# Pooled attention and a gated FFN on one core: the first keys and queries loaded by SyncE as float32 and cast on the engines, conv weights by ScalarE's queue, wrap copies over two blocks, and a new order

## The chip, the cores and the metric

The kernel runs on one core of one Trainium2 chip. The metric is the device time of one execution in microseconds (us). Three runs of the kernel before gave 217.94, 218.74 and 219.59 us.

## The reference, cut to what matters

Shapes: q, k, v are float32 [8, 8, 576, 64] (batch, heads, sequence, head size); the FFN has `w_in` [512, 1024], `conv_w` [3, 1024], `w_out` [1024, 512]; the result is float32 [8, 576, 512].

```python
# attention over keys and values that are averaged in groups of 8 positions
k_p = k.reshape(B, H, 72, 8, D).mean(axis=3)
v_p = v.reshape(B, H, 72, 8, D).mean(axis=3)
scores = scale * q @ k_p.T
scores = scores - scores.max(-1)
attn = exp(scores) / (exp(scores).sum(-1) + 1e-9)
x = (attn @ v_p)                       # heads joined: [B, 576, 512]
# gated FFN
h = maximum(x @ w_in, 0)               # [B, 576, 1024]
conv = conv_w[0] * h[s-1] + conv_w[1] * h[s] + conv_w[2] * h[s+1]
out = (h * sigmoid(conv)) @ w_out
```

## The kernel before

The eight batches are taken in four groups of two. Each batch goes through the same stages. Its keys are pooled and turned (`prep_k` by TensorE with a pooling matrix for batches 0 and 1; `pool_pair` by VectorE adds and `turn_pair` for the later groups). Its queries are turned (`prep_q`, or a transposing DMA for the last group). Its values are pooled by VectorE (`prep_v`). Attention runs in tiles of 128 rows (`att_scores`, `att_max`, `att_shift`, `att_exp`, a turn of the exponentials, `att_values`, `att_divide`, a turn of x). Then come `ffn_in` (line 712), relu on ScalarE (721), the convolution over positions, tanh, the gate, and `ffn_out` (928) with stores. The convolution is done on TensorE by small matmuls with diagonal matrices `dw` (874) for most quarters, and on VectorE by three taps (849) for six of them.

Positions lie in a strided order (position = 9 p + c), so that the neighbour of a row is a shift by 64 columns, except at the ends of the tile. For batches 4 to 7 the two wrapped column blocks at the ends of `hT` are written by GpSimd copies (`ffn_wrap`, lines 796 and 797) so that convolution reads one straight run. `Graph.WRAPS` says for how many of the 128-channel blocks one pair of copies is done.

What sets the order: every operation is added to a graph with its engine and costs. `Graph.ORDER`, a table of numbers, is the order in which the operations are emitted; an odd number picks the second of the two engines that could do a copy. A -1 is a spare matmul on zeros (`fill`, line 384) that only keeps TensorE busy. `FORMS` picks between two matmul shapes for some operations, and `PLACES` gives each operation its buffer. Each engine then works through its own list strictly in that order, and waits by semaphores for what other engines deliver. Costs and landing times in the `add` calls serve the making of the table, which was written into the file; they are not read on the chip.

What the change touches in the kernel before:

- All q, k and v loads, `w_in` and `w_out` are issued by GpSimd, whose DMAs cast float32 to bf16 on the way (`load_heads`, line 272). The first keys come in two halves of the heads (`kk`, 128x2x576), the first queries in two parts of the columns (`qp`, 128x4x256 and 128x4x320). GpSimd also builds the mask, the identity and, by two selects of line 316, the pooling matrix `pm`, which VectorE then doubles (332).
- The conv weights are loaded by SyncE (line 297), turned by one small matmul (365), and made into `convw` and `dw` by VectorE.
- `clear_ends` (lines 791 and 792) zeroes the two outer columns of both `hT` buffers on GpSimd.

Of the kernel before, what the change touches and what calls it, by code (L numbers as in the profile page):

```python
# [33 lines left out]
class Graph:  # L34
# [27 lines left out]
    WRAPS = 4  # L62
# [60 lines left out]
    )  # L123
    FORMS = (
        0, 1, 0, 1, 0, 1, 1, 0, 0, 0, 0, 0, 1, 1, 1, 0, 0, 0, 0, 0, 0, 1, 1, 0, 0, 0, 0, 0, 0, 0, 0, 1, 1, 1, 0, 1, 1, 1, 1, 1,
    )
    PLACES = (
# [50 lines left out]
def kernel(  # L178
# [102 lines left out]
    def load_q(b, **part):  # L281
        load_heads(buf("qp", b), q, b, **part)
# [707 lines left out]
    def soon():  # L990
        seq[0] += 0.01
        return seq[0]
# [400 lines left out]
```

## Time and profile before

| | |
|---|---|
| runs of the kernel | 217.94, 218.74, 219.59 us; median 218.74 |
| the profiled execution | 219.76 us, of which the span of instructions is 218.0 us, the rest lies around it |
| mean granted TensorE clock | 0.997 |
| busy: PE, DVE, ACT, POOL | 200.7, 194.2, 158.6, 39.1 us |
| HBM read, written | 32.52 MB, 9.44 MB |

The profile is of one execution. PE is TensorE, DVE VectorE, ACT ScalarE, POOL GpSimd, SP SyncE. "Busy" is the time in which an engine had an instruction in work; matmuls overlap, so a busy PE isn't PE at its peak. "Landing" is the time from a DMA's issue to the arrival of its last data. The DMA columns give the mean busy share of the 16 DMA engines and the bytes that they wrote per second; a load that casts reads twice the bytes that it writes.

### The profile page before, as it was taken

The page shows a single profiled execution, that of the slowest core. Times are in us where ns is not written, and L with a number is a line of the kernel's source. Part 1 is how long each engine was busy: PE and PEld are TensorE (multiplying, and loading weights), DVE is VectorE, ACT ScalarE, POOL GpSimd, SP SyncE. Part 2 cuts the span into 40 slices and gives each one's busy share as a digit, 9 for nine tenths or more (in the row PEclk, how much of TensorE's full clock was granted, in tenths as well). Part 3 has the DMA queues.
Part 4 walks back from the last instruction along what each step waited for, and adds up shares of the span by engine and source line. Part 5 has one row for each costly group of instructions (what it writes and reads, how often), then busy time and mean ns, then how long its engine had stood idle before and what let it go on. Part 6 is the DMA issues. An engine that isn't in the chain of part 4 may idle for free.

```text
span 218.0 us, 6525 instructions
## 1 busy us (share of the span) xinstructions
PE 200.7 (92%) x2718; PEld 136.8 (63%) x2718; DVE 194.2 (89%) x339; ACT 158.6 (73%) x269; POOL 39.1 (18%) x65
## 2 busy tenths in 40 slices
PE   2798999997999999999999998999999999999991
PEld 1465778774688776856777765566556656654451
DVE  7569879999999998999999997999999999999531
ACT  2046676798989868867786985699599989988410
POOL 7951422042042012000000012002010120321000
PEclk9999999999999999999999999999999999999998
DMA  4999999999999999984956895476564555401886
GB/s 70 141 191 208 208 206 208 206 208 205 210 225 207 206 149 183 143 165 92 168 119 88 129 101 108 99 143 117 113 144 89 129 110 121 100 0 36 197 255 189
DMA packets 48833, 32.61 MB, mean 150 GB/s; under 512 B 28300, under 2 KB 44324, under 8 KB 48804
## 3 DMA queue, kind: packets, MB, share of 16 engines
q0 software_dynamic: 16288, 16.26, 46.3%
q1 hardware_dynamic: 31476, 14.44, 34.6%
q10 hardware_dynamic: 1040, 1.51, 2.4%
q8 instruction: 21, 0.34, 0.6%
q14 instruction: 8, 0.07, 0.1%
HBM read 32.52 MB, written 9.44 MB: 192 GB/s over the span
## 4 chain that ended last, share of the span: by engine, by line
PE 44%; DVE 31%; DMA 11%; issue 6%; POOL 5%; ACT 2%; DVEq 0%; POOLq 0%
PE psum L928 19%; PE psum L712 14%; DMA w_in_sb<-in_moe_w_in_dram 9%; DVE negm L593 6%; DVE x L682 5%; DVE sd L605 4%; PE psum L874 4%; DVE tg L849 4%; DVE gT L912 3%; PE psum L667 3%; DMA eT<-e 2%; DVE v L471 2%; DVE gT L920 2%; DVE r L680 2%; POOL qp L272 1%
## 5 line engine op out<-in xcount | busy, mean ns | idle before, releaser
L712 PE MATMUL psum<-xT,w_in_sb 128*128 128x288 bf16 x512 | 73.6, 286 | 0.8 <-DVE sd L605 0.3
L928 PE MATMUL psum<-w_out_sb,gT 128*128 128x512 bf16 (+1 forms) x296 | 69.8, 373 | 1.2 <-DVE gT L920 0.7
L712 PEld LDWEIGHTS <-w_in_sb 128*128 128x128 bf16 x512 | 47.9, 98 | 17.4 <-issue 1.0
L721 ACT ACTIVATE hT<-psum 128x576 bf16<-128x576 f32 x64 | 40.1, 651 | 12.2 <-PE psum L712 12.0
L928 PEld LDWEIGHTS <-gT 128*128 128x128 bf16 x296 | 27.3, 98 | 26.4 <-issue 1.5
L849 DVE SCALAR_TENSOR_TENSOR tg<-hT,convw,tg 128x576 f32<-128x576 bf16 x48 | 37.4, 816 | 0.5
L593 DVE TENSOR_REDUCE negm<-psum 128x8 f32<-128x576 f32 (+2 forms) x37 | 27.4, 751 | 3.2 <-PE psum L580 2.7
L682 DVE TENSOR_TENSOR x<-psum,r 128x512 bf16<-128x512 f32 (+1 forms) x37 | 25.6, 691 | 1.3
L796 POOL COPY hT<-hT 128x252 bf16<-128x252 bf16 x8 | 4.5, 559 | 100.1 <-ACT hT L721 90.9
L667 PE MATMUL psum<-vm,eT 128*128 128x130 bf16 (+5 forms) x240 | 19.2, 222 | 2.1 <-DMA eT<-e 1.3
L605 DVE TENSOR_TENSOR sd<-psum,negm 128x576 f32<-128x576 f32 x27 | 20.0, 752 | 0.5
L874 PE MATMUL psum<-hT,dw 64*64 64x288 bf16 (+2 forms) x608 | 19.3, 261 | 1.0 <-issue 0.4
L667 PEld LDWEIGHTS <-eT 128*128 128x128 bf16 (+1 forms) x240 | 15.3, 101 | 6.1 <-DMA eT<-e 1.8
L631 ACT ACTIVATE e<-sd 128x576 bf16<-128x576 f32 x27 | 18.1, 682 | 1.3 <-DVE sd L605 1.0
L874 PEld LDWEIGHTS <-dw 64*64 64x64 bf16 x608 | 15.0, 107 | 5.4 <-issue 4.2
L854 ACT ACTIVATE gT<-tg 128x576 bf16<-128x576 f32 x24 | 16.2, 687 | 2.7 <-DVE tg L849 2.6
L847 ACT ACTIVATE tg<-hT,convw 128x576 f32<-128x576 bf16 x24 | 18.0, 780 | 0.1
L939 ACT COPY osb<-psum 128x512 f32<-128x512 f32 x26 | 14.8, 587 | 4.1 <-PE psum L928 4.0
L899 ACT ACTIVATE tg<-psum 128x576 bf16<-128x576 f32 x20 | 13.0, 648 | 4.4 <-PE psum L874 3.7
L899 ACT ACTIVATE gT<-psum 128x576 bf16<-128x576 f32 x20 | 13.0, 648 | 3.4 <-PE psum L874 3.1
L920 DVE TENSOR_TENSOR gT<-gT,hT 128x2304 bf16<-128x2304 bf16 x10 | 13.5, 1351 | 0.1
L471 DVE TENSOR_TENSOR v<-v 128x1280 bf16<-128x1280 bf16 (+2 forms) x24 | 13.0, 540 | 0.1
(82 smaller groups left out, 230.2 us busy)
## 6 DMA issues: line engine op xcount, KB each, us to landing
out_dram<-osb SPq DMA_DIRECT2D x54, 128.0 KB, 2.4
v<-in_v_dram POOLq DMA_DIRECT2D x8, 512.0 KB, 14.5
qp<-in_q_dram POOLq DMA_DIRECT2D x7, 576.0 KB, 15.2
kk<-in_k_dram POOLq DMA_DIRECT2D x3, 1152.0 KB, 14.4
out_dram<-qp ACTq DMA_DIRECT2D x10, 128.0 KB, 2.8
w_in_sb<-in_moe_w_in_dram POOLq DMA_DIRECT2D x2, 512.0 KB, 17.6
w_out_sb<-in_moe_w_out_dram POOLq DMA_DIRECT2D x1, 1024.0 KB, 23.8
out_dram<-qp SPq DMA_DIRECT2D x6, 128.0 KB, 2.6
```

The lines of the kernel that those rows point to most:

```text
L593: nc.vector.tensor_reduce(out=a["m"][0:rows], in_=a["s"][0:rows, :, 0:2 * KW].rearrange("p a (h s) -> p a h s", s=Sp), axis=AX.X, op=OP.ma ...
L605: nc.vector.tensor_tensor(out=a["d"][0:rows], in0=a["s"][0:rows, :, 0:2 * KW].rearrange("p a (h s) -> p a h s", s=Sp), in1=a["m"][0:rows]. ...
L631: nc.scalar.activation(out=dst, in_=src, func=ACT.Exp, scale=1.0 / (POOL * 8.0),)
L667: nc.tensor.matmul(out=a["o"][lo:hi, h // 4, (h % 4) * (D + 1):(h % 4 + x1 - x0) * (D + 1)], lhsT=a["eT"][:, j, lo:hi], rhs=buf("vm", b)[: ...
L682: nc.vector.tensor_tensor(out=a["x"][0:rows].rearrange("p (a h d) -> p a h d", a=2, d=D), in0=ov[:, :, :, 0:D], in1=r[0:rows].unsqueeze(3) ...
L712: nc.tensor.matmul(out=banks(ps)[:, j, 0:SC], lhsT=w_in_block(dc, fb), rhs=buf("xT", g)[:, dc, i * S + j * SC:i * S + (j + 1) * SC], start ...
L721: nc.scalar.activation(out=h_of(b)[:, fb].rearrange("p (a s) -> p a s", a=2), in_=banks(ps)[:, :, 0:SC], func=ACT.Relu, scale=0.5,)
L847: nc.scalar.activation(out=acc, in_=h, func=ACT.Identity, scale=w)
L849: nc.vector.scalar_tensor_tensor(out=acc, in0=h, scalar=w, in1=acc, op0=OP.mult, op1=OP.add)
L874: nc.tensor.matmul(out=banks(pss[r ^ c])[c * D:(c + 1) * D, j, lo:hi], lhsT=dw[r * D:(r + 1) * D, tap * n_fb + fb, :], rhs=hT[r * D:(r + 1 ...
L899: nc.scalar.activation(out=t.rearrange("p (a s) -> p a s", a=2), in_=banks(ps)[:, :, 0:SC], func=ACT.Tanh, scale=0.5,)
L928: nc.tensor.matmul(out=bank(ps)[0:rows, columns], lhsT=buf("gT", g)[:, fb, t * P:t * P + rows], rhs=w_out_sb[:, fb, columns], start=(fb == 0),
```

## The change

The first keys and the first part of the first queries are no longer loaded by GpSimd. SyncE loads them uncast, as float32, into the two `hT` buffers, which are not in use yet (`load_raw`), and four copies cast them to bf16 into their old places (`cast_raw`): one half of the keys on VectorE, the other half and two halves of the query part on ScalarE. Of the first queries the second part stays with GpSimd, but waits in the graph for the pooling matrix. The conv weights are issued from ScalarE's queue and their turning matmul stands later. `clear_ends` comes after the four casts, since the staging lies in `hT`. `WRAPS` goes from 4 to 2. `ORDER`, `FORMS` and `PLACES` are new throughout.

```diff
-    WRAPS = 4
+    WRAPS = 2
...
-        24, 2, 6, 28, 36, 4, 26, 18, 8, 16, 10, -1, 14, 20, -1, -1, 34, 54, -1, 12,
+        0, 10, 12, 24, 16, -1, 4, 44, -1, 28, 8, -1, 36, -1, 14, -1, -1, 32, -1, -1,
...
+    def raw_rows(i):
+        flat = buffers["hT"][i].rearrange("p a s -> p (a s)").bitcast(FP32)
+        return flat[:, 0:H // 2 * C * D].rearrange("p (h x) -> p h x", h=H // 2)
+
+    def load_raw(i, heads, cs):
+        rows = (k, q)[i][0].rearrange("h s d -> (h s) d").rearrange("(h p c) d -> p h c d", p=P, c=C)
+        nc.sync.dma_start(
+            out=raw_rows(i)[:, heads, cs.start * D:cs.stop * D].rearrange("p h (c d) -> p h c d", d=D),
+            in_=rows[:, heads, cs],
+        )
+
+    def cast_raw(i, heads, cs, copy):
+        part = slice(cs.start * D, cs.stop * D)
+        copy(out=(k_rows_of(0), buf("qp", 0))[i][:, heads, part], in_=raw_rows(i)[:, heads, part])
...
-        nc.sync.dma_start(out=cw_raw, in_=cw)
+        nc.scalar.dma_start(out=cw_raw, in_=cw)
...
+        if b == 0 and (kind == "k" or part["cs"].start == 0):
+            heads, cs = part.get("heads", slice(0, 4)), part.get("cs", slice(0, C))
+            d = add({"SP": 0.5}, key, lambda: load_raw(raw, heads, cs), land=(0.6, kb * share, RATE_FIRST))
+            cast = []
+            for lo in range(heads.start, heads.stop, 2):
+                two, n = slice(lo, lo + 2), 2 * D * (cs.stop - cs.start)
+                o = add(either(0.145 + n * 0.00056, 0.25 + n * 0.00085), key, None, after=[d], uses=[toks[b]])
+                o.emit = lambda o=o, two=two: cast_raw(raw, two, cs, copier(o))
...
+    ends = add({"POOL": 0.8}, 0, clear_ends, after=raws)
...
-    add_load("q", 0, first("q0+"), 5 / 9, cs=slice(4, C))
+    add_load("q", 0, first("q0+"), 5 / 9, [p0], cs=slice(4, C))
```

The start of GpSimd's list, after the constants, before:

```order
6 L272 DMA kk_76<-in_k_dram 128x2x576
7 L335 MEMSET mask 128x15
8 L337 ISA
9 L337 AFFINE_SELECT mask<-mask 128x15 x2
10 L272 DMA kk_76<-in_k_dram 128x2x576
11 masks.py:197 MEMSET ident 128x128
12 masks.py:199 AFFINE_SELECT ident<-ident 128x128
13 L272 DMA qp_72<-in_q_dram 128x4x256
14 L272 DMA qp_72<-in_q_dram 128x4x320
15 L316 AFFINE_SELECT gT_120<-gT_120 64x9x72 x2
16 L290 DMA v_85<-in_v_dram 128x4x512
```

The same place after the change (line numbers of the changed kernel, where the lines from 297 on stand 15 or more further down):

```order
6 masks.py:197 MEMSET ident 128x128
7 masks.py:199 ISA
8 masks.py:199 AFFINE_SELECT ident<-ident 128x128
9 L350 MEMSET mask 128x15
10 L352 AFFINE_SELECT mask<-mask 128x15 x2
11 L331 AFFINE_SELECT gT_120<-gT_120 64x9x72 x2
12 L272 DMA qp_72<-in_q_dram 128x4x320
13 L305 DMA v_85<-in_v_dram 128x4x512
14 L308 DMA v_85<-in_v_dram 64x512
15 L272 DMA kk_76<-in_k_dram 128x4x576
16 L272 DMA qp_73<-in_q_dram 128x4x576
```

Three loads have left GpSimd's list, and the mask, identity and pooling matrix now stand ahead of its first load. Further on the first half of `w_in` stands ahead of batch 2's queries, where it stood behind them.

VectorE's list around the copy that doubles the pooling matrix, before:

```order
21 L349 TENSOR_SCALAR vm_88<-mask 128x15
22 L349 TENSOR_SCALAR vm_89<-mask 128x15
23 L349 TENSOR_SCALAR vm_90<-mask 128x15
24 L349 TENSOR_SCALAR vm_91<-mask 128x15
25 L349 TENSOR_SCALAR vm_92<-mask 128x15
26 L332 COPY gT_120<-gT_120 64x9x72
27 L354 COPY mask_wide<-mask 128x960
28 L416 COPY kT_80<-psum 64x2x72 x3
```

And after the change:

```order
15 L364 TENSOR_SCALAR vm_91<-mask 128x15
16 L364 TENSOR_SCALAR vm_92<-mask 128x15
17 L327 MEMSET kT_80 128x288
18 L369 COPY mask_wide<-mask 128x960
19 L294 COPY kk_76<-hT_114 128x1152
20 L347 COPY gT_120<-gT_120 64x9x72
21 L431 COPY kT_80<-psum 64x2x72 x2
22 L534 COPY qT_77<-psum 128x2x256
```

The wide mask and the cast of the first keys now stand ahead of the doubling copy (347, before 332), and six memsets of `e` and the four copies of `pick`, which stood ahead of it, stand behind it.

SyncE's list at its start, before:

```order
1 L297 DMA gT_120<-in_moe_conv_w_dram 24x128
2 L951 DMA out_dram<-osb_121 64x512 x2
3 L651 DMA_TRANSPOSE eT_102<-e_96 128x5x128
4 L951 DMA out_dram<-osb_122 64x512 x2
5 L513 DMA_TRANSPOSE qT_77<-qp_73 128x18x128
6 L951 DMA out_dram<-osb_123 64x512 x2
7 L651 DMA_TRANSPOSE eT_104<-e_97 128x5x128
```

And after the change:

```order
1 L287 DMA hT_114<-in_k_dram 128x2x576
2 L287 DMA hT_115<-in_q_dram 128x4x256
3 L287 DMA hT_114<-in_k_dram 128x2x576
4 L666 DMA_TRANSPOSE eT_103<-e_97 128x5x128
5 L666 DMA_TRANSPOSE eT_104<-e_96 128x5x128
6 L528 DMA_TRANSPOSE qT_77<-qp_73 128x18x128
7 L966 DMA out_dram<-osb_121 64x512 x2
8 L966 DMA out_dram<-osb_122 64x512 x2
9 L966 DMA out_dram<-osb_123 64x512 x2
```

The three new loads come first, and the first stores of results now stand behind the large transposing DMA of batch 6's queries (528, before 513).

More of the change, by code (lines that the diff above doesn't have):

```diff
@@ L70 @@
     ORDER = (
[52 rows of a table removed]
[52 rows of a table added]
     )
     FORMS = (
-        0, 1, 0, 1, 0, 1, 1, 0, 0, 0, 0, 0, 1, 1, 1, 0, 0, 0, 0, 0, 0, 1, 1, 0, 0, 0, 0, 0, 0, 0, 0, 1, 1, 1, 0, 1, 1, 1, 1, 1,
+        1, 0, 1, 0, 1, 1, 1, 0, 0, 0, 0, 1, 1, 0, 0, 1, 1, 0, 0, 0, 0, 1, 1, 0, 0, 0, 0, 1, 0, 0, 0, 1, 1, 1, 1, 0, 1, 1, 1, 1,
     )
     PLACES = (
[17 rows of a table removed]
[17 rows of a table added]
     )
@@ L983 @@
     LATE = 1.4
-    RATE, RATE_FIRST = 402e3, 341e3
+    RATE, RATE_FIRST = 402e3, 395e3
     seq = [START]
@@ L992, in soon, with add_load @@
         return seq[0]
-    loads = {}
+    loads, raws = {}, []
     kk, kp, qp, qTt = {}, {}, {}, {}
     kb = B and H * S * D * 4
-    def add_load(kind, b, key, share=1.0, **part):
-        f, toks = (load_k, kp) if kind == "k" else (load_q, qp)
+    def add_load(kind, b, key, share=1.0, after=(), **part):
+        f, toks, raw = (load_k, kp, 0) if kind == "k" else (load_q, qp, 1)
         if kind == "k":
@@ L1003, in add_load @@
             toks[b] = token("qp", b)
-        o = add({"POOL": 0.77}, key, lambda: f(b, **part), uses=[toks[b]],
-                land=(0.5 if key == first("k0") else 1.3, kb * share, RATE_FIRST) if b == 0 else (LATE, kb, RATE))
+        if b == 0 and (kind == "k" or part["cs"].start == 0):
[6 more added lines that the diff above has]
+                o.emit = lambda o=o, two=two: cast_raw(raw, two, cs, copier(o))
+                cast.append(o)
+                raws.append(o)
+            loads.setdefault((kind, b), []).append(cast if kind == "q" else cast[0])
+            return
+        o = add({"POOL": 0.77}, key, lambda: f(b, **part), uses=[toks[b]], after=after,
+                land=(1.3, kb * share, RATE_FIRST) if b == 0 else (LATE, kb, RATE))
         loads.setdefault((kind, b), []).append(o)
@@ L1009 @@
     lv, vtok, vmtok, ktok = {}, {}, {}, {}
-    ends = add({"POOL": 0.8}, 0, clear_ends)
     def add_load_v(b, key):
@@ L1025 @@
     add_load("k", 0, first("k0+"), 0.5, heads=slice(2, 4))
-    cwl = add({"SP": 0.6}, soon(), load_conv, land=(1.5, 0, 1))
+    cwl = add({"ACT": 0.6}, soon(), load_conv, land=(7.0, 0, 1))
     cb0 = add({"DVE": 0.25}, soon(), lambda: nc.vector.memset(blank, 0.0))
@@ L1140, in add_prep_q @@
                 o = add({"PE": 0.52 * n / C}, key_q + half * gap + 2.2 * part, None,
-                        after=[loads["q", b][part], c0, idf], behind=[qfirst.get(b - 1)], count=4 * n, uses=[t, qp[b], qTt[b]], mode=HALF)
+                        after=[loads["q", b][part][half] if b == 0 and part == 0 else loads["q", b][part], c0, idf], behind=[qfirst.get(b - 1)], count=4 * n, uses=[t, qp[b], qTt[b]], mode=HALF)
                 o.emit = lambda o=o, half=half, part=part, t=t: prep_q(b, half, part, t, o.mode)
```

136 rows, old and new, of tables (ORDER, PLACES) are left out of this document.

## The prediction

> **What bounds the kernel now.** I read the busy shares first, then the stages, then who was waited for in the first stage.
>
> ```profile
> PE 200.7 (92%) x2718; PEld 136.8 (63%) x2718; DVE 194.2 (89%) x339; ACT 158.6 (73%) x269; POOL 39.1 (18%) x65
> DMA  4999999999999999984956895476564555401886
> 8.00:16.00 8.00, 6.79 (x133) 4.91 (x133) 5.29 (x10) 2.59 (x5) 5.76 (x9) 1.00 1.21 177
> ...
> 24.00:32.00 8.00, 7.29 (x141) 5.52 (x140) 6.63 (x13) 5.45 (x10) 2.21 (x3) 1.00 1.24 206
> 32.00:40.00 8.00, 8.00 (x113) 6.62 (x115) 7.65 (x15) 4.99 (x8) 1.32 (x2) 1.00 1.23 207
> 40.00:80.00 40.00, 37.42 (x637) 28.77 (x626) 39.00 (x71) 36.04 (x63) 8.73 (x15) 1.00 1.20 202
> 80.00:160.00 80.00, 77.33 (x1173) 53.38 (x1173) 76.82 (x127) 60.37 (x102) 5.17 (x9) 1.00 0.77 128
> 160.00:200.00 40.00, 39.73 (x288) 24.24 (x289) 39.10 (x54) 37.75 (x64) 6.68 (x10) 1.00 0.39 88
> ```
>
> The stage rows give the window, its length, then the busy time of PE, PEld, DVE, ACT and POOL, the granted clock, the DMA share and GB/s. From 32 us to 200 us DVE is busy for 162.6 of 168 us, and PE nearly as long. There, what starts later ends later; little can be hidden. Before 32 us there are holes, and the DMA engines are full from the second slice of the span on (5 us). So the first stage is the place to look, and its question is whether data come late. The rows of the engines, each with the start and the duration, say yes:
>
> ```profile
> 10.70 0.64 PE L501 MATMUL psum<-ident,qp 128*64 128x128 bf16 x16 [0.94 <-DMA qp<-in_q_dram]
> 12.63 0.75 POOL L290 DMA_DIRECT2D v<-in_v_dram  x1
> DMA to landing us min/median/max: 20.2/20.2/20.2
> 33.23 1.71 DVE L471 TENSOR_TENSOR v<-v 128x1280 bf16<-128x1280 bf16 x3
> 20.84 1.03 POOL L279 DMA_DIRECT2D kk<-in_k_dram  x1 [4.77 <-PE psum L401]
> DMA to landing us min/median/max: 18.0/18.0/18.0
> 39.43 2.63 DVE L424 TENSOR_TENSOR kk<-kk 128x2304 bf16<-128x2304 bf16 x3
> ```
>
> The landing rows belong to the load quoted ahead of each. Batch 1's values land at 12.63 + 20.2 = 32.8, and DVE takes them up at 33.23. The second group's keys land at 20.84 + 18.0 = 38.8, and DVE takes them up at 39.43. The first queries keep PE waiting until 10.70. Up to 39 us the line of loads sets the pace, because the work that uses each load begins within 0.7 us of its landing. **If that line moves, the program moves.**
>
> **What the change does to the line of loads.**
>
> ```profile
> 1.32 0.85 POOL L272 DMA_DIRECT2D kk<-in_k_dram  x1 [0.80 <-POOLq L1377]
> 0.81 0.43 SPq L297 DMA_DIRECT2D gT<-in_moe_conv_w_dram  x1
> 1.80:2.00 0.20, 0.00 (x0) 0.00 (x0) 0.15 (x1) 0.20 (x1) 0.20 (x1) 1.00 0.22 59
> 2.80:3.00 0.20, 0.00 (x0) 0.00 (x0) 0.20 (x1) 0.00 (x0) 0.20 (x2) 1.00 0.51 46
> 3.00:9.00 6.00, 4.57 (x28) 2.20 (x29) 4.15 (x23) 0.36 (x2) 5.86 (x10) 1.00 1.02 134
> 9.00:10.00 1.00, 0.75 (x19) 0.58 (x18) 0.61 (x3) 0.21 (x1) 1.00 (x2) 1.00 1.27 167
> 206.00:208.00 2.00, 2.00 (x11) 0.87 (x9) 0.00 (x0) 1.07 (x2) 0.00 (x0) 1.00 1.00 286
> 214.00:216.00 2.00, 0.00 (x0) 0.00 (x0) 0.07 (x1) 0.00 (x0) 0.00 (x0) 1.00 0.96 316
> ```
>
> SyncE's load issued at 0.81 moved its 12 KB within 1.8 to 2.0 us (59 GB/s in that window). GpSimd's first load, issued at 1.32, moved its first data from about 2.8 us. So SyncE's loads begin about 1.0 us earlier.
>
> Now the three moved loads. As bf16 they are 2 x 295 KB and 262 KB, 0.852 MB written. Before, 6 us at 134 GB/s make 0.804 MB by 9.0, 0.009 MB came ahead of that, and the rest comes at 167 GB/s: they are through, counted by bytes, at 9.2 us. After, they are written as float32, 1.704 MB. Uncast traffic from the hardware queues is seen only at the end, in the stores: 286 to 316 GB/s with the engines full. At these rates the three take 5.4 to 6.0 us and end at 7.2 to 7.8 us, so **the line is 1.4 to 2.0 us ahead**. Bounds from other rows: a saturated casting load writes 208 GB/s and so reads 416; at 416 the three end at 5.9, 3.3 us ahead. If the written side were the limit at 208 GB/s, they would end at 10.0, 0.8 us behind; at the start's own 134 GB/s they would end at 14.5, 5.3 us behind. The stores are nearest, being uncast float32 from the same kind of queue, but they are paced by PE in part, so I take 1.9, near the upper end of theirs.
>
> [...]
>
> Does the line then run on without a hole? GpSimd builds the identity, mask and pooling matrix first:
>
> ```profile
> 2.37 0.54 POOL L337 TENSOR_SCALAR_AFFINE_SELECT mask<-mask 128x15 bf16<-128x15 bf16 x2
> 3.88 0.29 POOL masks.py:199 TENSOR_SCALAR_AFFINE_SELECT ident<-ident 128x128 bf16<-128x128 bf16 x1
> 5.63 1.92 POOL L316 TENSOR_SCALAR_AFFINE_SELECT gT<-gT 64x648 bf16<-64x648 bf16 x2
> 3.62 0.24 DVE L1027 MEMSET gT<- 128x224 uint32 x1
> 5.09 0.33 DVE L329 MEMSET gT<- 64x324 uint32 x1
> ```
>
> Identity and mask take 1.3 us with their memsets, from 1.32 to 2.6. The selects need DVE's memsets; these took 3.62 to 5.42 before, 1.8 us, and now come first on DVE, so they end at 2.7. The selects end at 4.6, and the held load of queries is issued then; first data come 1.5 us later, at 6.1, while SyncE's loads still run to 7.2 or later. So no hole. Values, batch 1's keys and queries follow at once; then GpSimd waits for the casts (the four memsets of `clear_ends`) before it issues `w_in`. The casts end near 9.5 us (below), and the loads already issued, batch 1's queries as the last of them, landed past 18 us before and move by no more than the lead, so this wait is hidden; it costs only if ScalarE's cast came 9 us later. Behind it stand `w_in` and batch 2's queries.
>
> **The engines in the first 12 us.** DVE's list now reaches the doubling of the pooling matrix like this:
>
> ```profile
> 0.93 0.82 DVE L312 MEMSET v<- 64x256 uint32 x3 [0.93 <-PEq L1377]
> 3.03 0.29 DVE L312 MEMSET e<- 128x32 uint32 x6
> 5.59 0.48 DVE L349 TENSOR_SCALAR vm<-mask 128x15 bf16<-128x15 bf16 x5
> 7.58 0.34 DVE L332 COPY gT<-gT 64x648 bf16<-64x648 bf16 x1 [1.51 <-POOL gT L316]
> 7.95 1.15 DVE L354 COPY mask_wide<-mask 128x960 bf16<-128x960 bf16 x1
> 7.98 0.93 PE L391 MATMUL psum<-gT,kk 128*64 128x144 bf16 x18 [0.51 <-DVE gT L332]
> 12.03 0.41 PE L580 MATMUL psum<-kT,qT 128*128 128x144 bf16 x4
> ```
>
> Before, DVE ran from 0.93 to 6.07 and then waited 1.51 us for GpSimd's selects. Now that wait is gone, but the wide mask (1.15) and a cast of 1152 elements stand ahead, while the memsets of `e` (0.3) and four small copies of `pick`, taken as 0.3 too, left: 6.07 - 0.6 + 1.15 = 6.6, plus the cast. No row shows a cast of float32 in SBUF. It lies between a DVE copy of 1152 elements (0.75 us, below) and the 1.15 us for 960, stretched to 1152 (1.38). I take 1.0: the doubling copy starts at 7.6, as before. **The first key matmul gains nothing.** What gains is what follows. PE needn't wait until 10.70 for queries. ScalarE's cast of the second key half (1.1 us by the copy of 1152) ends near 9.5 us, 1.3 us after its data at about 8.2; the second key matmuls follow, then 28 query turns (1.0 us). The first scores come at about 11.4 instead of 12.03.
>
> ```profile
> L519 DVE COPY qT<-psum 128x1152 bf16<-128x1152 bf16 x4 | 3.0, 751 | 0.6 <-PE psum L667 0.6
> L519 ACT COPY qT<-psum 128x1152 bf16<-128x1152 bf16 x6 | 6.7, 1122 | 0.5 <-PE psum L501 0.4
> L656 DVE COPY eT<-psum 128x640 bf16<-128x640 bf16 x5 | 2.4, 484 | 0.0
> L797 POOL COPY hT<-hT 128x252 bf16<-128x252 bf16 x8 | 6.5, 810 | 0.0
> 85.39 7.95 SPq L513 DMA_TRANSPOSE qT<-qp  x1
> ```
>
> From there to batch 1's values four copies have left DVE for ScalarE or for later: queries of 1152 columns (0.75), queries and exponentials of 640 (0.48 each), exponentials of 320 (0.3 at that rate), 2.0 us together. With the 0.6 DVE can be 2.6 us ahead at 33 us, more than the loads' 1.9, so the loads still set the pace there. Past the second group's keys the DVE lists differ by two query copies more (1.50) and four other copies less (1.6): nothing. So a lead of 1.9 us at 39 us is passed on.
>
> The conv weights now land later, but are used only after the second tile's scores; the finer wrap copies double GpSimd's count from 16 to 32 at about half the length (810 ns for 252 columns), and GpSimd is 18% busy. Both cost nothing; if GpSimd were the last to be waited for, a wrap pair would come about 0.7 us sooner.
>
> **The sum.** 1.9 us off the span of 218.0 gives 216.1, off the profiled 219.76 gives 217.9. That execution is 1.0 us above the median of the runs, so against the median: 218.74 - 1.9 = **216.8 us**.
>
> **Rivals.**
> (a) The lead grows: the loads run at 416 GB/s and the new order closes holes. The 32 to 200 us rows leave 5.4 us of DVE idle. With 3.3 us from the loads and 1 us of holes, 214.4. For it: the casting loads do read at 416. Against: the two lists have the same structure.
> (b) The float32 writes limit the start. They are twice the bytes. Below 1.704 / (9.2 - 1.8) = 230 GB/s the line falls behind; at 134 it costs 5.3 us: 224.0. For it: 134 GB/s is what this very stage shows. Against: uncast stores go at 286 or more.
> (c) A new wait at SyncE. The transposing DMA that held SyncE for 7.95 us now stands ahead of three stores, and the second of its kind ahead of two sends of exponentials. If that one too takes 7.95, both tiles come late by 0 to 7.95 us; with buffers only three deep I take a little over the middle, 4.5: 218.74 - 1.9 + 4.5 = 221.3. It decides once those sends are needed sooner than the transposing DMA ends. For it: the row above. Against: TensorE and DVE have other tiles in work.
> (d) The change doesn't move the line: DVE's start, unmoved at 7.6, bounds all tiles of batch 0. Then only the 0.6 us count: 218.1.
>
> **How the numbers follow.** Forecast 0.45, (a) 0.20, (b) 0.08, (c) 0.15, (d) 0.12. About 1% (2.2 us) is what a measurement of this kernel can tell from no change; the limits are 216.55 and 220.93. The forecast's own range is 215.4 to 218.4; a little under half of it lies below 216.55 once reordering is allowed 1 us. Faster: 0.20 + 0.20 of the forecast's 0.45 = 0.40. Slower: (b) and 0.12 of (c)'s 0.15, 0.20. Same: the other 0.25 of the forecast, (d) and the rest of (c), 0.40. The range runs from 214.0, just past (a), to 221.0, just short of (c)'s price; outside it lie (b), about two thirds of (c), and a little below.
>
> **What would show it.** SyncE's loads through by 8 us; the first key matmul at 7.9 to 8.3; first scores at 11 to 11.8; batch 1's values taken up at 31.0 to 31.8 and the second group's keys near 37.5; the same DVE busy share after. Wrong, if the DMA rate before 8 us is under 230 GB/s, or if the lead at 39 us is there and gone at the end, which would put it on the new order.

## The result, and the profile after

The changed kernel takes 217.87 us (median of 20 runs, 216.11 to 219.22) beside 219.03 us for the kernel before (20 runs, 217.94 to 222.02). The ratio is 0.9947 with a 95% interval of 0.9928 to 0.9966: it is faster by 1.2 us, 0.5%. Ratios and their intervals leave out executions over 1.5% longer than the fastest of the same kernel, while medians are over all. A second study gave 217.00 us (6 runs) beside 220.05 us for the kernel before (23 runs) and a ratio of 0.9864 (0.9823 to 0.9904), which is 3.0 us. The two intervals do not meet: in the second study the changed kernel was 0.9 us faster and the kernel before 1.0 us slower. What the faster times go with stands below; why the kernel before was slower there, no run explains.

The busy shares and the clock of the profiled execution after (218.23 us, span 216.5):

```profile
PE 201.9 (93%) x2753; PEld 137.0 (63%) x2753; DVE 193.2 (89%) x334; ACT 162.7 (75%) x278; POOL 41.5 (19%) x78
PEclk9799999999999999999999999999999999999999
```

The second row is the granted TensorE clock in 40 slices of 5.4 us. Before, no slice but the last was under 9, as the row of the kernel before has it; now the second one is 7.

```profile
PEclk9999999999999999999999999999999999999998
```

The windows of the start (length, then PE, PEld, DVE, ACT, POOL busy, granted clock, DMA share, GB/s) show the loads and the clock together:

```profile
3.00:4.00 1.00, 1.00 (x4) 0.45 (x3) 0.93 (x4) 0.00 (x0) 1.00 (x2) 1.00 1.01 373
4.00:5.00 1.00, 1.00 (x5) 0.40 (x3) 0.93 (x5) 0.00 (x0) 1.00 (x2) 1.00 1.09 378
5.00:6.00 1.00, 0.80 (x5) 0.20 (x2) 1.00 (x7) 0.00 (x0) 1.00 (x3) 1.00 1.04 333
6.00:7.00 1.00, 0.00 (x0) 0.00 (x0) 1.00 (x2) 0.96 (x2) 1.00 (x2) 1.00 1.02 356
...
8.00:9.00 1.00, 1.00 (x26) 0.99 (x22) 0.16 (x1) 0.84 (x1) 0.00 (x0) 0.61 1.26 163
9.00:10.00 1.00, 0.87 (x17) 0.64 (x14) 0.15 (x1) 0.96 (x3) 0.63 (x5) 0.50 1.06 138
10.00:11.00 1.00, 1.00 (x24) 1.00 (x22) 0.30 (x1) 0.00 (x0) 1.00 (x3) 0.50 1.25 201
11.00:12.00 1.00, 1.00 (x34) 0.91 (x34) 0.89 (x9) 0.27 (x1) 1.00 (x2) 0.68 1.24 204
```

From 3 to 7 us 333 to 378 GB/s are written, more than the 286 to 316 of the stores. Up to about 5 us this is nearly all SyncE's float32: GpSimd's first casting load is issued at 3.59, and its data come about 1.5 us later if it is as before (issued at 1.32, first data at about 2.8). The last of SyncE's three loads is issued at 1.83 and lands 6.3 us later, at 8.1. From about 8.2 to 11.6 us, for 3.4 us, the clock is granted at half (0.50 over 9 to 11 us). TensorE's timeline shows what this does (start, duration, and in brackets the idle time ahead and what ended it):

```profile
1.23 4.57 PE L399 MATMUL psum<-gT 128*128 128x448 bf16 x14 [1.23 <-DVE gT L1052]
7.83 0.97 PE L406 MATMUL psum<-gT,kk 128*64 128x144 bf16 x18 [2.03 <-DVE gT L347]
9.37 1.29 PE L406 MATMUL psum<-gT,kk 128*64 128x144 bf16 x18
...
11.90 0.32 PE L582 MATMUL psum<-kT,qT 64*64 64x72 bf16 x16
```

Fills are the spare matmuls on zeros. Ahead of the key matmuls there are now fourteen, which start at 1.23 (nine from 3.92 before) and end at 5.80, 2.03 us before the first key matmul (0.51 before). The second key half takes 1.29 us instead of 0.75. The first scores start at 11.90 instead of 12.03. What came of the data, as rows of the engines with the landing of the load quoted ahead:

```profile
8.16 1.15 ACT L294 CAST kk<-hT 128x1152 bf16<-128x1152 f32 x1 [0.99 <-DMA hT<-in_k_dram]
6.59 0.74 DVE L294 CAST kk<-hT 128x1152 bf16<-128x1152 f32 x1
9.37 0.14 POOL L806 MEMSET hT<- 128x8 bf16 x1 [1.73 <-ACT kk L294]
11.71 0.77 POOL L305 DMA_DIRECT2D v<-in_v_dram  x1
DMA to landing us min/median/max: 18.0/18.0/18.0
31.82 1.70 DVE L486 TENSOR_TENSOR v<-v 128x1280 bf16<-128x1280 bf16 x3
18.35 1.03 POOL L279 DMA_DIRECT2D kk<-in_k_dram  x1 [4.95 <-PE psum L416]
DMA to landing us min/median/max: 17.4/17.4/17.4
36.75 1.35 DVE L439 TENSOR_TENSOR kk<-kk 128x2304 bf16<-128x2304 bf16 x1
86.85 2.97 SPq L528 DMA_TRANSPOSE qT<-qp  x1
```

Batch 1's values land at 11.71 + 18.0 = 29.7 us, 3.1 us sooner than before, but VectorE takes them up at 31.82, only 1.4 sooner. The second group's keys land at 35.75 and are taken up at 36.75. **The line of loads moved, and it no longer sets the pace.** What the engines did ahead of batch 1's values shows it, in the changed kernel (first row) and in the kernel before (the other two):

```profile
31.15 0.76 DVE L534 COPY qT<-psum 128x1152 bf16<-128x1152 bf16 x1 [0.84 <-PE psum L520]
30.34 0.66 PE L712 MATMUL psum<-xT,w_in_sb 128*128 128x288 bf16 x4 [0.16 <-DMA w_in_sb<-in_moe_w_in_dram]
32.29 0.95 DVE L376 TENSOR_TENSOR dw<-ident,convw 128x768 bf16<-128x768 bf16 x1
```

In the changed kernel VectorE waits for TensorE just before it takes up the values. In the kernel before it had work of its own (`dw`) until 33.24, and until 39.5 ahead of the second group's keys, so it waited for neither load there. What the loads did hold up before the change was TensorE, by 0.94 us at 10.70 (the first queries) and by 0.16 us at 30.34 (`w_in`). So the engines' own work was close behind the loads already.

The later stages of the changed kernel, to be held against the three stage rows from 40 us on in the prediction:

```profile
40.00:80.00 40.00, 37.07 (x607) 28.48 (x605) 39.27 (x70) 35.05 (x63) 8.25 (x11) 1.00 1.16 192
80.00:160.00 80.00, 77.43 (x1163) 52.10 (x1162) 76.46 (x126) 61.28 (x105) 7.90 (x18) 1.00 0.73 125
160.00:200.00 40.00, 40.00 (x298) 24.40 (x297) 38.36 (x52) 36.88 (x63) 8.91 (x16) 1.00 0.47 105
200.00:216.00 16.00, 12.25 (x65) 6.04 (x63) 5.93 (x10) 4.05 (x8) 0.00 (x0) 1.00 0.70 197
```

And the last stage of the kernel before:

```profile
200.00:216.00 16.00, 13.61 (x88) 6.78 (x76) 7.44 (x11) 4.41 (x8) 0.00 (x0) 1.00 0.83 227
```

From 40 to 200 us TensorE is busy for 154.48 us before and 154.50 after. What it has left at 200 us is 13.61 and 12.25 us: the 1.4 us that it is ahead were there at 40 us, and are the gain in the span (218.0 to 216.5). VectorE is further ahead (its take-up of the second group's keys is 2.7 us sooner), but TensorE is full from 160 us on, so VectorE's surplus buys nothing.

### The profile page after: what moved, and what is told of

Read it like the earlier page. It is cut to its first block, busy times and chain, and to the rows that moved or that the text cites. A ratio compares the mean times of both kernels' runs of the same rounds, so it can differ in the third digit from the quotient of the medians.

```text
span 216.5 us, 6617 instructions
## 1 busy us (share of the span) xinstructions
PE 201.9 (93%) x2753; PEld 137.0 (63%) x2753; DVE 193.2 (89%) x334; ACT 162.7 (75%) x278; POOL 41.5 (19%) x78
## 4 chain that ended last, share of the span: by engine, by line
PE 45%; DVE 34%; issue 6%; ACT 6%; DMA 5%; SPq 2%; DVEq 0%
PE psum L943 20%; PE psum L727 16%; DVE negm L608 7%; DVE x L697 6%; DVE sd L620 4%; DVE gT L935 4%; DMA hT<-in_k_dram 3%; DVE v L486 3%; DVE gT L927 3%; PE psum L889 2%; DMA out_dram<-osb 2%; DVE r L695 2%; PE psum L682 2%; ACT e L646 2%; DVE gT L925 1%
## 5 line engine op out<-in xcount | busy, mean ns | idle before, releaser
L811 POOL COPY hT<-hT 128x126 bf16<-128x126 bf16 x16 | 7.5, 467 | 97.6 <-ACT hT L736 80.1
L954 ACT COPY osb<-psum 128x512 f32<-128x512 f32 x27 | 15.7, 585 | 4.4 <-PE psum L943 4.2
L889 PE MATMUL psum<-hT,dw 64*64 64x288 bf16 (+2 forms) x608 | 18.7, 261 | 0.1
```

What stands on the lines that cost most here:

```text
L889: nc.tensor.matmul(out=banks(pss[r ^ c])[c * D:(c + 1) * D, j, lo:hi], lhsT=dw[r * D:(r + 1) * D, tap * n_fb + fb, :], rhs=hT[r * D:(r + 1 ...
```

## The experiments

Theory "clock": the 2.03 us of idle before the key matmuls let the clock be halved, and TensorE can't make that up. Rival "order": the new order gives the lead back later, and the matmuls at half clock cost nothing. Each run was compared with the kernel before on the same chip. The experiments fall into three studies on three chips (the first four, the next four, the last four), and the kernel before differs between studies by up to 1.0 us; so differences inside a study count for more than those between studies. Edits are shown shortened.

**Ten more fills, up to the key matmuls.**

```diff
     def fill(ps):
-        nc.tensor.matmul(out=bank(ps)[:, 0:448], lhsT=blank[:, 0:P], rhs=blank, start=True, stop=True)
+        fills.append(ps)
+        for _ in range(11 if len(fills) == 14 else 1):
+            nc.tensor.matmul(out=bank(ps)[:, 0:448], lhsT=blank[:, 0:P], rhs=blank, start=True, stop=True)
```

> The changed kernel with ten more matmuls of the filling kind behind the fourteenth, so that TensorE works on from 5.8 us until the first key matmul at 7.8 us. Nothing else is changed, and the results aren't. Theory 'clock': the changed kernel's 2.03 us of idle before the key matmuls is what halved the granted clock from 8 to 11.7 us, and TensorE, which is nearly full to the end, can't make that up. Then the clock stays at 1.00 in these windows, the second half of the key matmuls takes 0.75 us instead of 1.29, the first scores start at 11.0 to 11.3 us instead of 11.90, and the time falls by 0.7 to 1.2 us against the changed kernel, to 216.7 to 217.2 us. Rival 'order': the lead of 2.4 to 2.7 us at 40 us is given back by the new order later (waits of SyncE near 120 and 139 us), and the slow matmuls lie in front of work that waits for loads anyway; the clock may be mended but the time stays within 0.3 us of 217.9.

216.31 us, ratio 0.9853 (0.9815 to 0.9891). The timeline of TensorE:

```profile
1.23 6.23 PE L403 MATMUL psum<-gT 128*128 128x448 bf16 x24 [1.23 <-DVE gT L1056]
9.83 0.75 PE L410 MATMUL psum<-gT,kk 128*64 128x144 bf16 x18 [1.01 <-ACT kk L294]
11.45 0.32 PE L586 MATMUL psum<-kT,qT 64*64 64x72 bf16 x16
```

The clock stays at 1.00 and the second key half takes 0.75. From its start to the first scores it is 1.62 us (11.45 - 9.83) instead of 2.53 (11.90 - 9.37). The scores come at 11.45, later than I expected, because the second key half landed 0.5 us later in this execution. The time fell by a little more than expected, against a changed kernel that was run in another study; against its second study the intervals overlap.

**GpSimd's loads in the new order.**

```diff
     def load_raw(i, heads, cs):
-        nc.sync.dma_start(...)
+        load_heads((k_rows_of(0), buf("qp", 0))[i], (k, q)[i], 0, heads, cs)
     def cast_raw(i, heads, cs, copy):
-        copy(...)
+        return
```

> The changed kernel in its new order, with the three first loads issued by GpSimd as casting loads, at the same places of the program, and no casts on VectorE and ScalarE. Theory 'line of loads': the gain comes from SyncE's early start and the float32 rate. GpSimd then issues the loads one after the other at about 0.8 us each between identity and mask, the line is behind by 1.5 to 2 us again, the second group's keys are taken up near 39 us, and the time is 219 to 220 us, as before the change or somewhat above it. Rival 'new order': the order of work past 12 us brings the gain, and the time stays at 217.5 to 218.3 us.

219.55 us, ratio 0.9992 (0.9965 to 1.0020): all of the gain is gone, as the first theory says. The kernel with ten fills in the same study has 0.9853.

The stage row of 16 to 24 us, and VectorE's timeline:

```profile
16.00:24.00 8.00, 6.01 (x127) 4.50 (x128) 5.92 (x14) 3.87 (x8) 3.06 (x4) 0.79 1.21 205
```

```profile
16.30 0.83 DVE L481 TENSOR_TENSOR v<-v 128x1280 bf16<-128x1280 bf16 x1 [1.96 <-DMA v<-in_v_dram]
34.91 1.34 DVE L481 TENSOR_TENSOR v<-v 128x1280 bf16<-128x1280 bf16 x2
```

VectorE waits 1.96 us for batch 0's values, and batch 1's are taken up at 34.91, 3.1 us behind the changed kernel. In the same stage the clock falls a second time (a mean of 0.79 over 16 to 24 us, after 0.88 over 0 to 14 us).

**SyncE's loads in the old order.** The loads of `load_conv`, `load_k` and `load_q` for batch 0 in the kernel before, and the casts ahead of the doubling copy:

```diff
     def load_conv():
+        load_raw(0, slice(0, 2))
+        load_raw(1, cs=slice(0, 4))
+        load_raw(0, slice(2, 4))
         nc.sync.dma_start(out=cw_raw, in_=cw)
     def double_pool_matrix():
+        cast_raw(0, slice(0, 2), slice(0, C), nc.vector.tensor_copy)
+        for lo in (0, 2):
+            cast_raw(1, slice(lo, lo + 2), slice(0, 4), nc.scalar.copy)
+        cast_raw(0, slice(2, 4), slice(0, C), nc.scalar.copy)
```

> The kernel before, in its old order, with only the three first loads moved to SyncE as float32 (conv weights behind them on SyncE), their casts put ahead of the doubling copy on VectorE and on ScalarE. Theory 'line of loads': SyncE's loads end near 8 us as in the changed kernel, GpSimd issues the rest of the queries about 1.5 us sooner and values 0.5 us sooner, and the lead at batch 1's values and the second group's keys is 1.2 to 2.2 us. The fills end nearly where the key matmuls begin, so the clock stays up: 217.0 to 217.9 us. Rival 'new order': the loads alone bring less than 0.4 us, 218.6 to 219.2 us.

219.59 us over all twelve runs, ratio 0.9963 (0.9922 to 1.0003): not told apart from no change by the time alone. The runs behind the ratio have a median of 219.12 us, which is in the rival's range and not in the theory's. The trace tells more:

```profile
11.83 0.79 POOL L309 DMA_DIRECT2D v<-in_v_dram  x1
DMA to landing us min/median/max: 18.5/18.5/18.5
32.60 1.71 DVE L497 TENSOR_TENSOR v<-v 128x1280 bf16<-128x1280 bf16 x3
```

Batch 1's values land at 30.3, 2.5 us sooner than before, and are taken up at 32.60, 0.6 us sooner. In the old order, too, the take-up follows the landing by a small part only, as the rows of the kernel before above let one expect; the first scores come at 12.22 here, no sooner than before. So the moved loads alone bring little in the old order: a gain is shown for the loads and the new start of the engines together.

**The second key cast on VectorE, with the ten fills.** As the first experiment, and in `ORDER`:

```diff
-        42, 46, -1, 26, 40, -1, 48, -1, 21, -1, 64, 19, -1, 2, -1, 38, 66, 7, 100, 116,
+        42, 46, -1, 26, 40, -1, 48, -1, 21, -1, 64, 19, -1, 2, -1, 38, 66, 6, 100, 116,
```

> The first of these kernels with the cast of the second key half on VectorE, which is idle there, instead of ScalarE. Theory 'clock': the cast takes 0.74 us instead of 1.15, so the second key matmuls begin at 8.9 instead of 9.37 and the first scores 0.3 to 0.4 us sooner than with the filling matmuls alone; the time is the same as theirs or up to 0.4 us less, since the loads set the pace up to 39 us. Rival 'order': no difference of more than 0.2 us from the changed kernel.

216.49 us, 0.9853 (0.9816 to 0.9889): the same time as with the fills alone. The scores came at 10.25, more than a microsecond sooner, but then batch 0's values were the wait:

```profile
12.87 0.83 DVE L490 TENSOR_TENSOR v<-v 128x1280 bf16<-128x1280 bf16 x1 [0.67 <-DMA v<-in_v_dram]
```

**No fills ahead of the key matmuls.**

```diff
     def fill(ps):
+        fills.append(ps)
+        if len(fills) <= 14:
+            return
         nc.tensor.matmul(out=bank(ps)[:, 0:448], lhsT=blank[:, 0:P], rhs=blank, start=True, stop=True)
```

> The changed kernel without its fourteen filling matmuls ahead of the first key matmul; TensorE does nothing until 7.8 us. Theory 'clock': in the changed kernel the fourteen are wasted, because the clock is halved again by the idle 2.03 us behind them; without them it starts halved and comes up after some 3.4 us of work, the time that the changed kernel spent at half clock, so first scores come at 11.8 to 12.2 us and the time is that of the changed kernel, 217.6 to 218.2 us. Rival 'fills still help': the clock stays low longer than there, first scores past 12.5 us and 218.6 us or more.

218.82 us, 0.9917 (0.9876 to 0.9958), spread over 216.3 to 220.4. My expectation missed the time, and the scores, too, came sooner than I said (11.50). A window of the start, and TensorE's timeline:

```profile
8.00:9.00 1.00, 1.00 (x21) 1.00 (x20) 0.00 (x0) 0.91 (x1) 0.03 (x1) 1.00 1.26 157
```

```profile
7.84 1.29 PE L411 MATMUL psum<-gT,kk 128*64 128x144 bf16 x18 [7.84 <-DVE gT L347]
120.89 1.15 PE L732 MATMUL psum<-xT,w_in_sb 128*128 128x288 bf16 x8 [1.80 <-DMA xT<-x]
```

The two key halves took 1.29 and 1.34 us, as the second one did at a granted 0.50 in the changed kernel (1.29, and 0.75 at 1.00), although the column says 1.00: in this trace it does not show what slowed TensorE's first matmuls. In the changed kernel's trace the first of the fourteen fills take 581 ns each and the last 352, and the column says 1.00 there too. The first scores and batch 1's values (31.41) come sooner than in the changed kernel's trace, so what it loses it loses later: TensorE waits 1.80 us for a transposing DMA of x at 120.89, and 1.15 us for the like in the changed kernel's trace. This run is inconclusive on the fills.

**Four more fills instead of ten.**

```diff
-        for _ in range(11 if len(fills) == 14 else 1):
+        for _ in range(5 if len(fills) == 14 else 1):
```

> The changed kernel with four more filling matmuls instead of ten, so that TensorE idles about 1.2 us before the key matmuls instead of 2.03 (changed) or 0.38 (bridged). In the bridged kernel a gap of 1.01 us ahead of the second key half did no harm. Theory 'clock, by the length of the gap': a gap of 1.2 us leaves the clock at 1.00 and the time is the bridged kernel's, 216.0 to 216.8 us. Rival 'clock, by any gap in front of light work': halved again from about 8 us and 217.5 to 218.2 us as in the changed kernel.

217.10 us, 0.9870 (0.9832 to 0.9907). The gaps were 1.28 and 1.35 us, the clock 1.00, and the second key half took 0.75. Gaps of this length are survived here. The time lies between the two theories.

**The changed kernel again**, with no edit.

> The changed kernel unchanged, to stand beside the others of this call on one chip: 217.5 to 218.2 us, and the granted clock at 0.5 to 0.6 from 8 to about 11.7 us again if the halving is a property of the program and not of one execution. By the rival that the halving is chance, the clock is 1.00 there in this trace.

217.00 us, 0.9864 (0.9823 to 0.9904), less than I expected, and the rival was right: in this execution the clock stayed up. A window of the start, and TensorE's timeline:

```profile
9.00:10.00 1.00, 0.34 (x10) 0.34 (x12) 0.00 (x0) 1.00 (x3) 0.33 (x5) 1.00 1.08 137
```

```profile
7.83 0.75 PE L406 MATMUL psum<-gT,kk 128*64 128x144 bf16 x18 [1.87 <-DVE gT L347]
9.66 0.75 PE L406 MATMUL psum<-gT,kk 128*64 128x144 bf16 x18 [0.85 <-ACT kk L294]
11.28 0.33 PE L582 MATMUL psum<-kT,qT 64*64 64x72 bf16 x16
```

The same program, a gap of 1.87 us, and no halving; scores at 11.28. So the halving belongs to the execution, not to the program alone. Every run gives a mean granted clock, and 3.4 us at half of 216 lower it by 0.008. Of the 20 runs of the first study 16 lie under 0.995, of the 6 of this one 1. Over all 26, the 9 with a clock of 0.995 or more have a median of 217.01 us, and the 17 others 217.92. That mixes two studies; inside each it is 0.7 us (217.28 and 217.94 in the first, 217.00 and 217.69 in this one). **The executions with the lower clock are 0.7 us longer.** That the halving at the start makes the whole difference is not shown. The kernel before has no halving there in its trace, and yet 12 of its 63 runs beside the experiments lie under 0.995 and are 1.6 us longer (221.03 and 219.45): a low mean clock may also come of a wait elsewhere, as in the trace of GpSimd's loads with more fills (below).

Of the 18 runs of the three kernels with more fills, 17 are at 0.995 or more. In this study, where 5 of the 6 runs of the changed kernel keep their clock too, four more fills (217.10) bring nothing, as one would expect if fills help by the clock alone.

**GpSimd's first load not held back.** The load of the rest of the queries and the selects of the pooling matrix exchange places in GpSimd's list:

```diff
-    p0 = add({"POOL": 1.6}, first("pm"), build_pool_matrix, after=[c1])
+    p0 = add({"POOL": 1.6}, first("pm"), lambda: load_q(0, cs=slice(4, C)), after=[c1])
...
+    loads["q", 0][-1].emit = build_pool_matrix
```

> The changed kernel with GpSimd's first load (the rest of the queries) issued before the pooling matrix's selects instead of behind them, at about 2.0 us instead of 3.59; the selects follow 0.9 us later. Theory 'shared engines': the early load shares the 16 DMA engines with SyncE's three, so the second key half lands about 0.5 to 1 us later than 8.13, first scores come at 12.3 to 12.9 us, and the time is 0.3 to 0.8 us above the changed kernel. Rival 'no matter': the rest of the queries and all that follows on GpSimd's queue come sooner by as much, values of batch 1 are taken up no later than 31.8 us, and the time is the same within 0.2 us.

218.18 us, 0.9921 (0.9891 to 0.9951).

```profile
8.85 1.15 ACT L294 CAST kk<-hT 128x1152 bf16<-128x1152 f32 x1 [1.72 <-DMA hT<-in_k_dram]
10.05 1.29 PE L406 MATMUL psum<-gT,kk 128*64 128x144 bf16 x18 [1.24 <-ACT kk L294]
12.77 0.45 PE L582 MATMUL psum<-kT,qT 64*64 64x72 bf16 x16
32.78 1.70 DVE L486 TENSOR_TENSOR v<-v 128x1280 bf16<-128x1280 bf16 x3
```

The second key half was cast 0.7 us later, its matmuls met a halved clock (0.50 over 10 to 12 us) after gaps of 1.29 and 1.24 us, and batch 1's values were taken up at 32.78. The direction is that of the first theory. But the landing differs by as much between executions of kernels that hold the load back (below), and the ratio lies between the two of the changed kernel, so what the holding back is worth isn't settled.

**GpSimd's loads, with twelve more fills.** The second experiment, and in `fill`:

```diff
+        for _ in range(13 if len(fills) == 14 else 1):
```

> The kernel with GpSimd's casting loads in the new order, with twelve more filling matmuls so that TensorE works until its key matmuls at 8.3 us. Without them that kernel took 219.55 us with the clock halved from about 8.5 to 12 us in its trace. If the halving costs about 0.9 us in the executions that have it, this one takes 218.5 to 218.9 us, and what is left up to the bridged changed kernel, 2 us, is the moved loads' own gain, as forecast (1.9). Rival: the loads' loss was the clock's alone, and this one takes 217.5 us or less.

218.69 us, 0.9960 (0.9935 to 0.9985), as expected: 0.9 us less than without the fills, but the two were run in different studies and their intervals overlap.

```profile
12.98 0.25 PE L515 MATMUL psum<-ident,qp 128*64 128x128 bf16 x2 [2.06 <-DMA qp<-in_q_dram]
34.34 1.70 DVE L485 TENSOR_TENSOR v<-v 128x1280 bf16<-128x1280 bf16 x3
```

Here TensorE waits 2.06 us for queries, and the clock falls behind that wait after all (0.72 over 12 to 16 us). Against ten fills with SyncE's loads, in another study, it is 2.4 us by the medians. Against the three kernels with SyncE's loads of its own study (217.01 to 217.73, below) it is 1.0 to 1.7 us, and 1.7 against the one of them that has more fills too. So with more fills on both sides the moved loads are worth 1.7 to 2.4 us, this later halving among it.

**Conv weights on SyncE's queue.**

```diff
-        nc.scalar.dma_start(out=cw_raw, in_=cw)
+        nc.sync.dma_start(out=cw_raw, in_=cw)
```

> The changed kernel with the conv weights issued by SyncE, third behind its other loads, instead of ScalarE. The forecast costs this part at nothing: the same time as the changed kernel in its two studies, 0.986 to 0.995 of the kernel before, and the same first scores. Rival: ScalarE's issue delays its casts or the 12 KB delay the second key half, and it is 0.3 us or more off.

217.73 us, 0.9917 (0.9887 to 0.9947), between the changed kernel's two studies, so nothing of this part can be seen; 0.3 us, the rival's limit, would not be seen either. The scores came at 12.14, later than in the changed kernel's traces, with the clock halved (0.50 over 10 to 12 us).

**The wide mask behind the doubling copy.** The three operations exchange places in VectorE's list:

```diff
-    p1 = add({"DVE": 0.35}, soon(), double_pool_matrix, after=[p0])
+    p1 = add({"DVE": 0.35}, soon(), lambda: widen_mask(), after=[p0])
...
-    hmw = add(dve(1.15), soon(), widen_mask, after=[hm])
+    hmw = add(dve(1.15), soon(), lambda: cast_raw(0, slice(0, 2), slice(0, C), nc.vector.tensor_copy), after=[hm])
+    raws[0].emit = double_pool_matrix
```

> The changed kernel with VectorE's wide mask (1.09 us) behind the first key cast and the doubling copy instead of ahead of them. The data of the first key half are there at 4.4 us, so the first key matmul comes at 6.8 us instead of 7.83. Theory 'second key half': first scores hang on the second half's landing (8.1 to 9.0 us), so they do not move by themselves; the gap behind the filling matmuls shrinks to 1.0 us, so the clock is halved in fewer executions, and the time is between the changed kernel's and the bridged one's. Rival 'VectorE's list': the first key half was the bound and first scores come 0.7 us or more sooner, near 10.5 us.

217.12 us, 0.9893 (0.9863 to 0.9923).

```profile
7.67 1.15 ACT L294 CAST kk<-hT 128x1152 bf16<-128x1152 f32 x1 [0.62 <-DMA hT<-in_k_dram]
8.87 0.75 PE L406 MATMUL psum<-gT,kk 128*64 128x144 bf16 x18 [1.04 <-ACT kk L294]
10.49 0.32 PE L582 MATMUL psum<-kT,qT 64*64 64x72 bf16 x16
```

The first key matmul came at 6.86 as expected, and the scores at 10.49, which was the rival's number. But the rows give it another reason: the second half landed at 7.67 in this execution, TensorE sat idle for 1.04 us until its cast was done, and again it is 1.62 us from there to the scores. The second half bounds them, not VectorE's list.

**All three together**: the edit above, `66, 6, 100` in `ORDER`, and five more fills (`range(6 ...`).

> All that helped: five more filling matmuls, the wide mask behind the doubling copy, and the second key cast on VectorE. First scores at 10.0 to 10.6 us at full clock. Theory: what counts up to 32 us is TensorE's start, and from 160 us on TensorE is full, so the time is that of the bridged kernel or up to 0.4 us less, 0.983 to 0.986 of the kernel before. Rival: with the start 1.5 us sooner the loads' line sets the pace again at batch 1's values (data from 29.7 us on), and nothing more is gained.

217.01 us, 0.9888 (0.9862 to 0.9913): no better than the fills alone. Scores at 10.43, batch 0's values waited for by 0.95 us, batch 1's taken up at 31.31. The rival was right in the main: below about 11 us of first scores the loads are the bound again, though it is batch 0's values and not batch 1's that are waited for.

## Why the prediction was right or wrong

In one table, from the traces: the start of the second key half on TensorE, the time from it to the first scores, the first scores, and the take-up of batch 1's values.

| kernel | second half | to scores | scores | batch 1's values | difference |
|---|---|---|---|---|---|
| changed, first study | 9.37 | 2.53 | 11.90 | 31.82 | 19.92 |
| changed, again | 9.66 | 1.62 | 11.28 | 31.21 | 19.93 |
| ten fills | 9.83 | 1.62 | 11.45 | 31.36 | 19.91 |
| four fills | 10.16 | 1.62 | 11.78 | 31.70 | 19.92 |
| not held back | 10.05 | 2.72 | 12.77 | 32.78 | 20.01 |
| mask behind | 8.87 | 1.62 | 10.49 | 30.92 | 20.43 |
| ten fills, VectorE's cast | 8.63 | 1.62 | 10.25 | 30.85 | 20.60 |
| all together | 8.81 | 1.62 | 10.43 | 31.31 | 20.88 |
| no fills | 9.29 | 2.21 | 11.50 | 31.41 | 19.91 |
| conv weights on SyncE | 9.42 | 2.72 | 12.14 | 32.18 | 20.04 |
| GpSimd's loads | 9.76 | 2.55 | 12.31 | 34.91 | 22.60 |
| GpSimd's loads, more fills | 9.94 | 3.72 | 13.66 | 34.34 | 20.68 |

- **The line of loads set the pace before, and it moved: right in part.** The moved loads are the gain; without them it is gone (0.9992 beside 0.9853 in one study, 0.9960 beside 0.9888 in another). But I took "begins within 0.7 us of its landing" for a wait. VectorE waited for neither load in the kernel before; TensorE did for two others, by 0.94 and 0.16 us. The three moved loads ended at 8.1 us, past my 7.2 to 7.8, and still 2.5 us ahead: before, the last of them had landed at 10.6 (issued at 4.12, 6.5 us to landing), not at the 9.2 that I had counted by bytes. Batch 1's values landed 3.1 us sooner, not 1.9.
- **"The loads still set the pace" at 33 us: wrong, and this is the step that failed.** I had VectorE up to 2.6 us ahead there and took the loads for the later of the two. In the new order with SyncE's loads batch 1's values are taken up 19.9 to 20.0 us after the first scores, as long as the scores come after about 11 us; when they come sooner, waits for batch 0's values of 0.67 to 0.95 us fill the difference. With GpSimd's loads it is longer (22.60 with a wait of 1.96 us for batch 0's values, and 20.68). The bound passed from the loads to the engines' chain out of the second key half. That is rival (d)'s mechanism, though not its instance: it isn't the doubling copy at 7.6 us that bounds, but the second key half's landing, its cast and the clock. Nor is a lead of VectorE at 39 us passed on to the end, as I had it: 2.7 us there became 1.5 of the span, since TensorE, 1.4 us ahead, is full from 160 us on.
- **First scores at 11.4: right in executions with a full clock** (11.28, and 11.45 and 11.78 with more fills), wrong by 0.5 in the profiled one (11.90). I had not looked at what the fills' earlier end would do. TensorE's 2.03 us of idle were in the order that I read, and I gave them no price.
- **The size.** Forecast 216.8 against 218.74, 1.9 less; measured 1.2 less in the first study and 3.0 in the second. In the first study 16 of 20 executions had the lower clock. The four others have a median of 217.28, 1.75 us under the kernel before. So a term that I put at nothing is the clock at TensorE's start: 0.9 us at the first scores (2.53 against 1.62 in the table), and 0.7 us in the times of a study. The lead of the loads I took too small (1.9, measured 2.5 to 3.1), and what is passed on of it too large (all, measured about half). That these errors nearly cancel, and that the forecast lies between the two studies, is luck.
- **No hole behind the held load and `clear_ends` hidden: right; conv weights at nothing: no run speaks against it.** GpSimd waited 1.73 us for ScalarE's cast, and of the loads behind it the second half of `w_in` still landed at 27.2 us, before the first matmul on `w_in` at 27.48. Of the casts, VectorE's took 0.74 us (taken as 1.0) and ScalarE's 1.15 (taken as 1.1). The wrap copies were not tried by themselves.
- **Rival (b), float32 writes:** excluded by the 333 to 378 GB/s of the start.
- **Rival (c), SyncE:** the transposing DMA took 2.97 us in place of 7.95, so its price did not come due in this trace. SyncE's queue matters in another way: in the executions before and after, TensorE waits once or more for a transposing DMA, at different places.
  One row of TensorE's timeline before, and one of its weight loads after:

```profile
131.78 0.41 PE L667 MATMUL psum<-vm,eT 128*128 128x130 bf16 x4 [1.32 <-DMA eT<-e]
```

```profile
119.92 0.11 PEld L727 LDWEIGHTS <-w_in_sb 128*128 128x128 bf16 x2 [1.45 <-DMA xT<-x]
```

  Without fills such a wait was 1.80 us. These waits are as large as the effects studied here. Why they differ between executions and kernels stays open.

Of the versions tried, the one with ten more fills is the fastest by its median (216.31 us, 0.9853), and its interval is clear of no change and of the changed kernel's first study; from the changed kernel's second study it can't be told apart.

## What to carry to other kernels

When a load that sets the pace is moved, look up what is late next before passing its whole lead on: here the loads moved by 3.1 us and the work by 1.4, because the engines' own chain was only that far behind. A load that lands just before its use is no proof of a wait; the bracket in the row is. Where filler work keeps TensorE's clock up, as ten more fills did here (1.00 over 8 to 16 us), let it reach to the real work: where it ended 2 us too early, 17 of 26 executions had the lower clock, and the first scores came 0.9 us later behind a halving. And when two studies of one kernel differ by half a per cent, compare the granted clock of each run, and the kernel that both were held against, before the medians: here the kernel before makes about half of the difference.

## What the runs showed of the hardware

- **The clock was halved behind gaps of 1.2 to 2.1 us, and not always.** Behind a gap of 2.03 us it was halved from about 8.2 us on (0.50 over 9 to 11 us); behind one of 1.87 us it was not (1.00 over 5 to 16 us). Behind gaps of 1.29 and 1.24 us around 1 us of work it was (not held back, 0.50 over 10 to 12 us), and so it was behind gaps of 1.44 and 0.61 us (conv weights on SyncE, 0.50 over 10 to 12 us) and a wait of 2.06 us (GpSimd's loads with more fills, 0.72 over 12 to 16 us); behind gaps of 1.28 and 1.35 us after four more fills it was not (1.00 over 5 to 16 us). In each of the traces with a halving it comes to 3.4 us at half. The gap itself differs between executions: the same fourteen fills took 4.57 to 5.31 us. The length of the gap alone does not decide it, since 1.87 us, and 1.28 and 1.35 us, left the clock up, and 1.29 and 1.24 us did not; what does, no run shows.
- The second key half landed at 7.7 to 9.0 us in executions with the same three loads (ScalarE's casts start at 7.67, 8.16, 8.46, 8.62, 8.96), and the scores follow it.
- A cast of 128x1152 float32 in SBUF to bf16 costs VectorE 0.74 us, as a bf16 copy of the same shape out of PSUM does (0.75), and ScalarE 1.15 (1.12 for that copy).
